# Turning normed rows by DMA instead of on TensorE in a fused attention and feed-forward kernel

## The chip, the cores and the metric

The kernel runs on one core of a Trainium2 chip. The metric is device time in microseconds for one launch, the median over several runs. One execution was also taken by the hardware profiler; durations of single instructions come from it. The engines are named as in the profile: PE is TensorE's matmul side and PEld its weight loads, DVE is VectorE, ACT is ScalarE, POOL is GpSimd, SP is SyncE, which here only issues DMAs.

## What is computed

Attention over hash buckets (4 batches, 8 heads, 768 positions, head size 64), followed by RMS norm and a gated feed-forward layer over 3072 tokens of width 512:

```python
q_bits = (np.einsum('bhsd,dk->bhsk', q, proj) > 0)      # 6 bits, a bucket each; k likewise
mask = q_bucket[:, :, :, None] == k_bucket[:, :, None, :]
scores = np.where(mask, scale * np.matmul(q, k.transpose(0, 1, 3, 2)), -1e9)
attn = softmax(scores)                                  # over keys
x = np.matmul(attn, v)                                  # to tokens x 512
xn = x / rms * rms_g
g = xn @ w_gate                                         # 512 -> 1536
return (silu(g) * (xn @ w_val)) @ w_out                 # 1536 -> 512
```

Inputs and output are float32.

## The kernel before

**Units.** The work is cut into 8 units: unit u is one half (384 positions) of batch u // 2, with all 8 heads. A unit's attention has 24 slots (`SLOTS`): 8 heads by 3 blocks of 256 keys. In a slot PE makes two score tiles of 128 keys by 384 queries (line 369), ACT takes their exponential into `p` (line 376), and PE multiplies `p` with the values into `pv` a slot and a half later (line 400; the last slot of a head pair adds a constant term, line 388).

**Order by hand.** Nothing is scheduled by the tool. Every step is put in a list with a position, `at(pos, fn)`, positions being counted in slots; the list is sorted by position and the steps are then issued in that order, so it sets the order on each engine. Each engine works its own instructions in order. A unit's base is 24 times its number; its norm and feed-forward part are laid over the attention of the next unit, whose base is `base = SLOTS * (u + 1)`.

**Norm of a unit** (`queue_norm`): `rstd` at base + 0.6 (DVE line 464, then POOL line 468), then three `scale` steps, one for each 128 tokens, 0.35 slots apart (DVE line 475), which write the normed rows `xn`, 128 tokens by 512 columns in float16. The gates need them turned, `xnT`, with the 512 columns on partitions in 4 groups of 128. `tr(0)` and `tr(1)` do that: each is 6 transposes of 128x128 on PE into a PSUM tile `xtp` of the pool `ring` (line 488), which DVE (line 494) or ACT (line 496) copies to `xnT`. For units 1 to 6 `tr(0)` is put 3.7 slots behind `rstd`.

**Gates** (`queue_gates`): 12 steps of a unit, each with 4 matmuls for the gate `g_ps` and 4 for the value `v_ps` (line 527), tanh on ACT (line 536), and two operations on DVE (lines 544 and 553) into `ht`. Every one of these matmuls reads all 384 tokens of `xnT`. Their PSUM tiles come from `gvpool`, which has 3 banks; a gate uses two. Positions are given in steps of F = 24 / 18 slots behind the base: 4, 5, 6, 7, 10, 11 and so on to 17 for units 1 to 5, and 4.45 for the first of unit 6.

**Output** (`queue_out`): 6 steps a unit of 6 matmuls each (line 591), over the slots of the unit after, at F-steps 0, 1, 2, 3, 8 and 9 for units 0 to 5; ACT copies out (line 601) and SP sends the unit out in one DMA (line 607).

**The next batch's q and k.** SP loads them a head pair at a time (`load_qk`, lines 71 and 72, 4 buffers each); PE turns them (line 226), a hash matmul in four column tiles of 32 gives the bits (line 240), and SP puts the bits, 6 rows at a time, into the scores' operands with small DMAs from SBUF to SBUF (`place`, line 259, 8 for a head pair). For batches 2 and 3 the four loads stand at 8 and 3 slots before the base and 2 and 7 after it; PE uses them from slots 0.4, 10.3, 24.4 and 32.3 behind that base.

**Opening.** While the first loads are under way PE multiplies zeros (`keep_warm`, line 107): 24 matmuls of 128x128 into a scratch tile, and a few more between the first real steps. The first of these turns head 0 of q (line 226).

Of the kernel before, what the change touches and what calls it, by code (L numbers as in the profile page):

```python
# [8 lines left out]
FP32 = mybir.dt.float32  # L9
# [13 lines left out]
HQ = 384  # L23
NU = 2 * B
# [9 lines left out]
def kernel(  # L34
# [12 lines left out]
    nc = tc.nc  # L47
# [5 lines left out]
    ring = ctx.enter_context(tc.tile_pool(name="ring", bufs=4, space=PSUM))  # L53
    pvpool = ctx.enter_context(tc.tile_pool(name="pvpool", bufs=1, space=PSUM))
    gvpool = ctx.enter_context(tc.tile_pool(name="gvpool", bufs=3, space=PSUM))
# [4 lines left out]
    def at(pos, fn):  # L60
        queue.append((pos, len(queue), fn))
# [5 lines left out]
    def load_qk(b, hp):  # L67
        ql = stage.tile([128, 2, 6, D], FP32, name="ql", tag="ql")
        kl = stage.tile([128, 2, 6, D], FP32, name="kl", tag="kl")
        hs = slice(2 * hp, 2 * hp + 2)  # L70
        nc.sync.dma_start(out=ql, in_=q[b, hs].rearrange("h (p c) d -> p h c d", c=6))
        nc.sync.dma_start(out=kl, in_=k[b, hs].rearrange("h (p c) d -> p h c d", c=6))
        loads[(b, hp)] = [ql, kl]
# [27 lines left out]
    zero = work.tile([128, HQ], FP16, name="zero", tag="bits", bufs=4)  # L101
    nc.vector.memset(zero, 0.0)
    wps = pvpool.tile([128, HQ], FP32, name="wps", tag="pv")

    def keep_warm(n):
        for _ in range(n):
            nc.tensor.matmul(  # L107
                wps[:, 0:128], zero[:, 0:128], zero[:, 0:128], start=True, stop=True
            )

    keep_warm(24)
    ident = const.tile([128, 128], FP32, name="ident")
    make_identity(nc, ident)
    NQK = 6
# [4 lines left out]
    for i in range(2):  # L119
        t = const.tile([128, 6, H, 65], FP16, name=f"v16_{i}")  # L120
# [6 lines left out]
    for e in range(2):  # L127
        t = const.tile([128, 32], FP32, name=f"pj1_{e}")
# [26 lines left out]
    for i in range(2):  # L155
        t = const.tile([128, NP, 1, 2, 65], BF16, name=f"vsum{i}")
# [171 lines left out]
    def queue_prep(b, hp, p0, step, hlag=0.3, eng=None, dpos=None):  # L328
        part = make_prep(b, hp)
        if (b, hp) == (1, 1):  # L330

            for j in range(4):
                pos = (24.56, 24.57, 26.6, 27.6)[j]
                part(pos, "tr_mm", j, (gvpool, "gv"))
                part(max(pos, 25.2), "tr_ev", j, "vvaa"[j])
            ph = 29.3
        else:
            for j in range(4):
                part(p0 + step * j, "tr_mm", j)
                part(p0 + step * j, "tr_ev", j, eng)  # L340
            ph = p0 + step * 4 + hlag
        part(ph, "hash_mm")
        part(ph, "bits")
        for i, (c, e) in enumerate(PLACES):
            part(ph + 0.001 * (i + 1), "place", c, e)
        for i, (c, e) in enumerate([(0, 0), (1, 0), (1, 1), (0, 1)]):
            part((dpos or ph + 0.7) + 1.33 * i, "dims", c, e)
        return part, ph
# [108 lines left out]
    xnT_of = {}  # L457

    def queue_norm(u, p, sgap, gap):
        tl = {}  # L460

        def rstd():
            ms = work.tile([128, 3], FP32, name="ms", tag="ms")
            nc.vector.tensor_scalar(  # L464
                ms, ss_of[u, 0], 1.0 / DMODEL, 1e-6, op0=ALU.mult, op1=ALU.add
            )
            rs = work.tile([128, 3], FP32, name="rs", tag="rs")
            nc.gpsimd.tensor_tensor(rs, ms, mhalf, op=ALU.pow)  # L468
            tl["rs"] = rs
            tl["xn"] = work.tile([128, 3, DMODEL], FP16, name="xn", tag="xn", bufs=1)  # L470
            xnT_of[u] = work.tile([128, 4, HQ], FP16, name="xnT", tag="xnT")

        def scale(t):
            def go():
                nc.vector.scalar_tensor_tensor(  # L475
                    out=tl["xn"][:, t, :], in0=x_of[u][:, t, :],
                    scalar=tl["rs"][:, t : t + 1], in1=grow,
                    op0=ALU.mult, op1=ALU.mult,
                )
            return go  # L480

        def tr(j):
            def go():
                m = ring.tile([128, 2, HQ], FP16, name="xtp", tag="r")
                for t in range(3):
                    for i in range(2):
                        kt = 2 * j + i
                        nc.tensor.transpose(  # L488
                            m[:, i, 128 * t : 128 * t + 128],
                            tl["xn"][:, t, 128 * kt : 128 * kt + 128],  # L490
                            ident16,
                        )
                if j == 0:
                    nc.vector.tensor_copy(xnT_of[u][:, 0:2, :], m)
                else:
                    nc.scalar.activation(xnT_of[u][:, 2:4, :], m, AF.Copy)  # L496
            return go

        at(p, rstd)
        for t in range(3):  # L500
            at(p + sgap + 0.35 * t, scale(t))
        at(p + gap, tr(0))
        at(p + gap + 0.35, tr(1))

# [210 lines left out]
    def qk_at(pos, b, hp):  # L715
        at(pos, lambda: load_qk(b, hp))

    def v_at(pos, part, b, hp):

        if (b, hp) != (1, 0):  # L720
            at(pos, lambda: load_v(b, hp))
        part(pos + 0.3, "vcast")
        part(pos + 0.31, "vsum")
# [6 lines left out]
    for b in range(1, B):  # L730
        base = SLOTS * (2 * b - 1)
        if b == 1:
            p0s = (17.3, None, base + SLOTS + 0.4, base + SLOTS + 8.3)
        else:
            p0s = (base + 0.4, base + 10.3, base + SLOTS + 0.4, base + SLOTS + 8.3)
            for hp in range(4):
                qk_at(base - 8.0 + 5.0 * hp, b, hp)
        parts = [
            queue_prep(
                b, hp, p0s[hp], 1.0,  # L740
                eng="v" if b == 1 and hp < 2 else None,
                dpos=(32.2, 37.5)[hp] if b == 1 and hp < 2 else None,
            )
            for hp in range(4)
        ]
        if b == 1:
            vps = [18.1, 30.2, 34.0, 38.0]
        else:
            vps = [parts[hp // 2][1] + 0.1 + 1.5 * (hp % 2) for hp in range(4)]
        for hp in range(4):  # L750
            v_at(vps[hp], parts[hp][0], b, hp)

    for u in range(NU):
        queue_attention(u, SLOTS * u, 1.0, 1.1 if u == 0 else 0.0)
        p = SLOTS * (u + 1) + 0.6
        if u == 0:
            queue_norm(u, p, 1.0, 6.2)
        else:
            queue_norm(u, p, 1.0, 3.7 if u < NU - 1 else 5.0)
    F = SLOTS / 18.0  # L760
    steps = lambda base, js: [base + 0.15 + F * j for j in js]
    for u in range(NU):
        base = SLOTS * (u + 1)
        if u == 0:
            queue_gates(u, [base + 8.0 + 1.33 * j for j in range(12)], 1.33)
        else:
            js = [4.0 if u < NU - 2 else 4.45, 5, 6, 7, 10, 11, 12, 13, 14, 15, 16, 17] if u < NU - 1 else range(6, 18)
            queue_gates(u, steps(base, js), F, u == NU - 1)
        js = [0, 1, 2, 3, 8, 9] if u < NU - 2 else range(6)
        queue_out(u, steps(base + SLOTS, js), u == NU - 1)  # L770

    for _, _, fn in sorted(queue, key=lambda e: (e[0], e[1])):
# [31 lines left out]
```

## Time and profile before

| what | us |
|---|---|
| median of 3 runs | 353.16 (352.51 to 353.35) |
| the profiled execution, its own time | 352.91 |
| its span | 351.1 |
| PE busy | 342.9 |
| ACT busy | 239.2 |
| DVE busy | 233.2 |
| scores, line 369 | 94.5 |
| gate and value matmuls, line 527 | 156.4 |
| output matmuls, line 591 | 68.7 |
| the `scale` steps, line 475 | 16.6 |

The span goes from the first to the last instruction that the profiler saw; the execution's own time is 1.8 us more. Busy times of matmuls overlap in the pipeline, so a group's mean is longer than the time it takes in PE's stream; the chain that ended last gives the latter. The granted TensorE clock is 0.998 over the span. In the timeline a row merges instructions of one kind that follow each other: start, length, engine, line, output and inputs, count, and in brackets the idle time of the engine before it with what ended it. "SPq" rows are issues of DMAs on SP's queue, not the transfers.

### The profile page before, as it was taken

How to read it: one execution, taken by the hardware profiler on the slowest of the kernel's cores; microseconds unless marked ns; L12 is line 12 of the kernel's file. 1: busy time of each engine (PE TensorE's matmuls, PEld its weight loads, DVE VectorE, ACT ScalarE, POOL GpSimd, SP SyncE). 2: the span in 40 equal slices, each digit the busy share in tenths (PEclk: the TensorE clock that was granted, in tenths of full speed). 3: DMA queues.
4: the chain of work that ended last, by engine and by line, in shares of the span. 5: the costliest groups of instructions: out<-in, count | busy, mean ns of one | idle time of the engine just before them, and what ended most of it. 6: DMA issues, size and time to landing. Idle time of an engine off the chain costs nothing.

```text
span 351.1 us, 8105 instructions
## 1 busy us (share of the span) xinstructions
PE 342.9 (98%) x3108; PEld 214.7 (61%) x3108; DVE 233.2 (66%) x493; ACT 239.2 (68%) x547; POOL 70.3 (20%) x112
## 2 busy tenths in 40 slices
PE   8998999999999999999999999999999999999996
PEld 6555665666666666666656656666666655665653
DVE  5667888677574784766767675767758644575771
ACT  4868877777677676777777677676767676772421
POOL 3899700820000006050000005051000000000000
PEclk9999999999999999999999999999999999999999
DMA  7956999500028016200008206220002000200202
GB/s 249 377 176 89 201 252 206 127 2 4 2 74 292 2 65 211 95 1 3 6 3 271 93 3 183 96 90 2 8 1 95 0 2 2 91 2 1 91 0 90
DMA packets 24054, 31.21 MB, mean 89 GB/s; under 512 B 2096, under 2 KB 20944, under 8 KB 24016
## 3 DMA queue, kind: packets, MB, share of 16 engines
q1 hardware_dynamic: 17792, 25.65, 21.9%
q0 software_dynamic: 5824, 4.72, 8.9%
q8 instruction: 24, 0.39, 0.4%
q10 hardware_dynamic: 400, 0.34, 0.3%
q14 instruction: 14, 0.11, 0.1%
HBM read 28.58 MB, written 6.29 MB: 99 GB/s over the span
## 4 chain that ended last, share of the span: by engine, by line
PE 94%; DVE 2%; ACT 2%; issue 1%; ACTq 0%; DVEq 0%
PE v_ps L527 18%; PE o_ps L591 18%; PE g_ps L527 17%; PE s_ps L369 17%; PE pv L400 10%; PE trps L226 6%; PE hps L240 3%; PE xtp L488 1%; PE pv L388 1%; ACT p L376 1%; PE hps L269 1%; PE wps L107 1%; DVE x L417 1%; ACT xnT L496 0%; DVE qk L276 0%
## 5 line engine op out<-in xcount | busy, mean ns | idle before, releaser
L376 ACT ACTIVATE p<-s_ps 128x384 f16<-128x384 f32 x384 | 162.9, 496 | 53.4 <-PE s_ps L369 52.9
L369 PE MATMUL s_ps<-qk 71*128 71x384 f16 x384 | 94.5, 326 | 0.4 <-ACT xnT L496 0.2
L527 PE MATMUL v_ps<-xnT,wv 128*128 128x384 f16 x384 | 78.1, 326 | 1.1 <-DVE a L544 1.1
L527 PE MATMUL g_ps<-xnT,wg 128*128 128x384 f16 x384 | 78.3, 325 | 0.1
L544 DVE SCALAR_TENSOR_TENSOR a<-th,g_ps 128x384 f32<-128x384 f32 x96 | 53.1, 553 | 33.1 <-ACT th L536 31.6
L400 PEld LDWEIGHTS <-p 128*128 128x128 f16 x1152 | 59.4, 97 | 24.6 <-issue 2.2
L591 PE MATMUL o_ps<-wo,ht 128*128 128x512 f16 (+1 forms) x300 | 68.7, 370 | 0.0
L400 PE MATMUL pv<-v,p 128*128 128x65 f16 x1152 | 66.2, 193 | 0.9 <-DVE x L417 0.7
L536 ACT ACTIVATE th<-g_ps 128x384 f32<-128x384 f32 x96 | 48.0, 499 | 17.6 <-PE g_ps L527 15.7
L553 DVE TENSOR_TENSOR ht<-a,v_ps 128x384 f16<-128x384 f32 x96 | 53.1, 553 | 8.4
L527 PEld LDWEIGHTS <-wv 128*128 128x128 f16 x384 | 37.5, 98 | 26.3 <-issue 1.6
L527 PEld LDWEIGHTS <-wg 128*128 128x128 f16 x384 | 35.1, 97 | 22.8 <-issue 2.3
L591 PEld LDWEIGHTS <-ht 128*128 128x128 f16 x300 | 28.2, 97 | 26.4
L468 POOL TENSOR_TENSOR rs<-ms,mhalf 128x3 f32<-128x3 f32 x8 | 6.9, 860 | 172.6 <-DVE ms L464 172.6
L369 PEld LDWEIGHTS <-qk 71*128 71x128 f16 x384 | 28.2, 98 | 14.2 <-issue 6.9
L601 ACT ACTIVATE osb<-o_ps 128x512 f32<-128x512 f32 (+1 forms) x23 | 13.5, 588 | 23.9 <-PE o_ps L591 23.9
L304 POOL CAST v<-vl 128x768 f16<-128x768 f32 x16 | 13.3, 834 | 67.7 <-DMA vl<-in_v_dram 45.0
L416 DVE RECIPROCAL r<-pv 128x6 f32<-128x6 f32 x32 | 6.2, 195 | 31.0 <-PE pv L400 30.8
L235 DVE TENSOR_SCALAR kT<-trps 128x384 f32<-128x384 f32 x28 | 15.5, 552 | 11.7 <-PE trps L226 11.7
L233 ACT ACTIVATE qT<-trps 128x384 f32<-128x384 f32 x29 | 14.4, 496 | 9.1 <-PE trps L226 9.1
L475 DVE SCALAR_TENSOR_TENSOR xn<-x,rs,grow 128x512 f16<-128x512 f32 x24 | 16.6, 748 | 4.6 <-POOL rs L468 4.6
L430 DVE CUSTOM_DVE_ANT_0 sq<-x 128x512 bf16<-128x512 f32 (+2 forms) x33 | 18.9, 571 | 0.9
(68 smaller groups left out, 272.6 us busy)
## 6 DMA issues: line engine op xcount, KB each, us to landing
vl<-in_v_dram SPq DMA_DIRECT2D x16, 384.0 KB
ql<-in_q_dram SPq DMA_DIRECT2D x15, 384.0 KB
kl<-in_k_dram SPq DMA_DIRECT2D x15, 384.0 KB
out_dram<-osb SPq DMA_DIRECT2D x7, 768.0 KB
qk<-bits SPq DMA_DIRECT2D x112, 4.5 KB
wg<-in_moe_w_gate_dram POOLq DMA_DIRECT2D x4, 384.0 KB, 6.8
wv<-in_moe_w_val_dram POOLq DMA_DIRECT2D x4, 384.0 KB, 9.3
wo<-in_moe_w_out_dram POOLq DMA_DIRECT2D x4, 384.0 KB, 13.2
```

What stands on the lines that cost most here:

```text
L226: nc.tensor.transpose(m[:, i, :], src[:, i, :], ident)
L235: nc.vector.tensor_scalar_mul(dst, mm, DIM)
L369: nc.tensor.matmul(s_ps, qk[0:71, 2 + hh, 128 * jt : 128 * jt + 128], qk[0:71, hh, HQ * hf : HQ * hf + HQ], start=True, stop=True,)
L376: nc.scalar.activation(p, s_ps, AF.Exp, scale=SCL)
L400: nc.tensor.matmul(acc[:, t, hh, :], p[:, 128 * t : 128 * t + 128], v16s[b % 2][:, 2 * (jt % 3) + jt // 3, h, :], start=(n % 6 == 0 and i ...
L430: nc.vector.tensor_tensor_reduce(out=sq[:, lo:hi], in0=xs, in1=xs, scale=1.0, scalar=0.0, op0=ALU.mult, op1=ALU.add, accum_out=ss_of[u, pa ...
L475: nc.vector.scalar_tensor_tensor(out=tl["xn"][:, t, :], in0=x_of[u][:, t, :], scalar=tl["rs"][:, t : t + 1], in1=grow, op0=ALU.mult, op1=A ...
L527: nc.tensor.matmul(ps, w[:, kt, fs], xnT[:, kt, :], start=(kt == 0), stop=(kt == 3))
L536: nc.scalar.activation(th, tl[f][0], AF.Tanh, scale=0.5)
L544: nc.vector.scalar_tensor_tensor(out=a, in0=th, scalar=1.0, in1=g_ps, op0=ALU.add, op1=ALU.mult)
L553: nc.vector.tensor_mul(ht_of[u][f], a, v_ps)
L591: nc.tensor.matmul(acc, ht_of[u][f][:, 128 * t : 128 * t + 128], wo[:, f, lo:hi], start=(f == 0), stop=(f == 11),)
```

## The change

For units 1 to 6, `queue_norm` no longer issues `tr(0)` and `tr(1)`. Behind each `scale` step stands one transposing DMA on SP's queue that reads 128 tokens by 512 columns of `xn` in SBUF and writes them, turned, to `xnT` in SBUF. No PSUM tile, no PE instruction and no copy on DVE or ACT is left in it. Units 0 and 7 keep the transposes on PE. The gates of units 1 to 6 start one F-step later (unit 6: 0.55 of a step), and the later ones are closer together, ending at 17.2 steps in place of 17. The last two output steps of units 0 to 5 are a step later. The loads of q and k for batches 2 and 3 stand at 8 and 3.5 slots before the base and 4.5 and 9 after it.

In the opening, 12 of the 24 zeros are replaced: two rounds, each with two matmuls whose operands are 64 rows high and four that are 32 rows high, of 384 columns, each row tile with its own PSUM tile, followed by 2 of the old kind.

```diff
-    keep_warm(24)
+    keep_warm(8)
+    parts_of = [
+        (gvpool if g % 2 else ring).tile(
+            [128, HQ], FP32, name="wps", tag="gv" if g % 2 else "r"
+        )
+        for g in range(4)
+    ]
+    for _ in range(2):
+        for rows in (64, 32):
+            for g in range(128 // rows):
+                z = zero[rows * g : rows * g + rows]
+                nc.tensor.matmul(parts_of[g], z[:, 0:128], z, start=True, stop=True)
+        keep_warm(2)
...
+        def tr_dma(t):
+            def go():
+                nc.sync.dma_start_transpose(
+                    out=xnT_of[u][:, :, 128 * t : 128 * t + 128], in_=tl["xn"][:, t, :]
+                )
+            return go
+
         at(p, rstd)
         for t in range(3):
             at(p + sgap + 0.35 * t, scale(t))
+        if 0 < u < NU - 1:
+            for t in range(3):
+                at(p + sgap + 0.35 * t + 0.01, tr_dma(t))
+            return
         at(p + gap, tr(0))
         at(p + gap + 0.35, tr(1))
...
-                qk_at(base - 8.0 + 5.0 * hp, b, hp)
+                qk_at(base + (-8.0, -3.5, 4.5, 9.0)[hp], b, hp)
...
-            js = [4.0 if u < NU - 2 else 4.45, 5, 6, 7, 10, 11, 12, 13, 14, 15, 16, 17] if u < NU - 1 else range(6, 18)
+            js = [5.0, 5.9, 6.9, 7.9, 10.9, 11.8, 12.7, 13.6, 14.5, 15.4, 16.3, 17.2] if u < NU - 1 else range(6, 18)
             queue_gates(u, steps(base, js), F, u == NU - 1)
-        js = [0, 1, 2, 3, 8, 9] if u < NU - 2 else range(6)
+        js = [0, 1, 2, 3, 9, 10] if u < NU - 2 else range(6)
```

## The prediction

> **What bounds the kernel now.** I read the page first: busy time by engine, then the shares of the chain that ended last.
>
> ```profile
> PE 342.9 (98%) x3108; PEld 214.7 (61%) x3108; DVE 233.2 (66%) x493; ACT 239.2 (68%) x547; POOL 70.3 (20%) x112
> ...
> PE 94%; DVE 2%; ACT 2%; issue 1%; ACTq 0%; DVEq 0%
> ```
>
> TensorE is 94% of the chain; DVE and ACT have a third of the span free. What leaves PE's stream shortens the run by its pace on PE, and any wait put into that stream lengthens it in full.
>
> Next, the view of the tile xtp, the transposes' PSUM target:
>
> ```profile
> L488 PE MATMUL xtp<-ident,xn x96: 217/219/230, 43.9 to 322.8; 128*128 128x128 f16 x96
> L494 DVE COPY xnT<-xtp x8: 547/558/559, 44.8 to 322.7; 128x768 f16<-128x768 f16 x8
> L496 ACT ACTIVATE xnT<-xtp x8: 810/810/818, 45.4 to 323.0; 128x768 f16<-128x768 f16 x8
> ```
>
> The 219 ns is one pipelined matmul's length, not its price. The chain in order of time gives line 488 1.5% of the span, 5.27 us for 96 transposes: 0.055 us each.
>
> Then the timeline where unit 1 is normed (start, length):
>
> ```profile
> 76.95 2.08 DVE L475 SCALAR_TENSOR_TENSOR xn<-x,rs,grow 128x512 f16<-128x512 f32 x3 [0.53 <-POOL rs L468]
> ...
> 79.31 0.50 PE L488 MATMUL xtp<-ident,xn 128*128 128x128 f16 x6
> ...
> 81.37 0.81 PE L527 MATMUL g_ps<-xnT,wg 128*128 128x384 f16 x4
> ...
> 81.76 1.50 SPq L259 DMA_DIRECT2D qk<-bits  x2
> ```
>
> and of unit 6, where PE does wait for the ACT copy:
>
> ```profile
> 282.32 2.08 DVE L475 SCALAR_TENSOR_TENSOR xn<-x,rs,grow 128x512 f16<-128x512 f32 x3 [0.96 <-POOL rs L468]
> ...
> 284.71 0.50 PE L488 MATMUL xtp<-ident,xn 128*128 128x128 f16 x6
> ...
> 286.79 0.81 PE L527 MATMUL g_ps<-xnT,wg 128*128 128x384 f16 x4
> ```
>
> The reader is to see how little lies between the last xn row (79.03; 284.40) and the first gate: 2.3 us. Units 2 to 5 repeat unit 1 with the same spacings, 41.35 us apart.
>
> Last, the opening, and bytes moved just after the first place DMA:
>
> ```profile
> 1.18 2.74 PE L107 MATMUL wps<-zero 128*128 128x128 f16 x24 [1.18 <-DVE pj L129]
> ...
> 3.86 0.87 PE L226 MATMUL trps<-ident,ql 128*128 128x128 f32 x3
> ```
> ```profile
> 82.75:83.00 0.25, 0.25 (x8) 0.21 (x7) 0.25 (x1) 0.00 (x0) 0.00 (x0) 1.00 0.00 0
> 83.00:83.25 0.25, 0.25 (x4) 0.16 (x2) 0.25 (x1) 0.00 (x0) 0.00 (x0) 1.00 0.07 19
> ```
>
> PE goes from the zeros straight into the first transposes, so a longer opening is on the path. The place DMA (SBUF to SBUF) began to issue at 81.76; its bytes moved in the slice from 83.00 to 83.25, 1.24 to 1.49 us later. That is my nearest row for a transposing DMA.
>
> **The change, part by part.** The sum is made against the profiled execution, 352.91 us (span 351.1); the median of the runs is 353.16, so 0.25 is added at the end.
>
> *Transposes off PE.* Six units of 12: 72 x 0.055 = 3.95 us off the bound engine. The six DVE copies (0.56) and ACT copies (0.81) go too; off the chain these are worth nothing, save in unit 6. There, from 284.71 to 286.79, 2.08 us pass for work that runs elsewhere at 12 transposes 0.66, two PV groups 2 x 0.18, two pairs of scores 2 x 0.33 = 1.68; the other 0.40 is the wait for the ACT copy. It goes: -0.40. In unit 1 the same count leaves 0.1; I book nothing.
>
> *The new wait.* PE's first gate of a unit now waits for three transposing DMAs, and PE is in order: all of attention queues behind it. When is it reached? In the changed order, what stands between the output matmuls and that gate is PV, hash, a score pair, PV, a score pair, PV with its constant. From 79.31: 0.18 + 0.79 + 0.33 + 0.18 + 0.33 + 0.35 puts the gate at 81.47. In unit 6 it is PV, scores, PV, scores, PV with constant: 284.71 + 1.37 = 286.08. When does the last transpose land? Its xn row ends at 79.03; SP follows DVE by 0.03 (bits end 81.73, place 81.76); 1.24 to 1.49 for a small DMA; and 128 KB at the 337 to 418 GB/s of the last output DMAs, 0.31 to 0.39. So 80.6 to 80.95: covered by 0.5 to 0.9 us in units 1 to 5. In unit 6, 284.43 + 1.55 to 1.88 = 286.0 to 286.3: a wait of 0 to 0.2; I take 0.2. SP can keep up if an issue takes the 0.66 us of a place DMA, against 0.69 us per xn row. No row shows a transposing DMA; the far bound is the 6.8 us from issue to landing of the weight loads on POOL's queue: 79.06 + 6.8 is 4.4 late, 284.43 + 6.8 is 5.15 late, 27 us in all. I take the near row, since payload, memory and queue are its kind.
>
> [...]
>
> *SP's queue.* 18 DMAs more. Behind each three stand the next head pair's places (first at 81.76 in unit 1; SP would be free by 79.7) and loads. Two of the q/k loads go from 2 and 7 slots after the unit's start to 4.5 and 9, behind the transposes; their tiles are used from slot 24.4, some 35 us later at 1.72 us a slot. Output steps 4 and 5 go a step later; their DMA is waited for a unit later. Nothing for these; without that cover a late load would stall PE by its delay.
>
> *Gates closer together.* Gates 4 to 11 keep their end but start later: 0.9 of a step apart instead of 1. PE waits for DVE to free a gate bank twice now, 1.1 us in all, at most 0.7. Bounds: 0 (DVE has 34% free and loses a copy) and one 0.7 wait per unit, 4.2; I take 0.5, nearer to the present two in eight units.
>
> *The zeros.* 24 zeros take 2.74 us, 0.114 per 128 columns. Twelve of them become matmuls of 384 columns, in four groups of 2 or 4 row tiles. If the tiles of a group run at once, four passes of 0.34 replace 12 x 0.114: equal. If one after another, 12 x 0.34 less 1.37: +2.74. Row tiles show in no row; the nearest, the hash's column tiles, do run together (four within 0.03 us of each other). I take +0.3 for tile starts; it could be -0.5 if PE's pace (0.055 per 128 columns later) came sooner.
>
> Sum: -3.95 - 0.40 + 0.2 + 0.5 + 0.3 = -3.35. 352.91 - 3.35 + 0.25 = **349.8 us**.
>
> **The rivals.** *The transposes follow one another* (slower). If each transposing DMA starts only when the one before has landed, with 1.7 us each from 77.67, the third lands at 82.8: 1.3 late, and in unit 6 283.04 + 5.1 is 2.1 late. 5 x 1.3 + 2.1 = 8.7 in place of 0.2: 358.1. For it: three DMAs on one path, and xn rows come every 0.69. Against: SP's place DMAs go out 0.72 to 0.75 apart, though each moves 1.2 later. It decides from d us each where 5(3d - 3.80) + (3d - 3.04) exceeds the rest's gain of 3.55: d = 1.42.
>
> *Each transpose costs SP by its 128-column blocks*: 12 issues of 0.66 from 77.67, then 0.7 to land, 86.3: 4.8 late, unit 6 5.6, together 29.7: 379 us. For it: a place of 4.5 KB costs SP more (0.66) than a load of 384 KB (0.42), so issue isn't priced by bytes. Against: a load of 256 runs of 1.5 KB costs SP less than a place of 6 runs, so issue isn't priced by pieces in these rows.
>
> *Row tiles don't run together*: +2.74 for 0.3, 352.2. *Closer gates wait once each unit*: 4.2 for 0.5, 353.5. In both the change moves the time by less than can be told.
>
> **How the numbers follow.** A measurement of this kernel can't tell 0.3%, 1.06 us, from no change: faster is below 352.1, slower above 354.2. Forecast 0.50, its own range 348.3 (waits nil, opening -0.5) to 352; transposes one after another 0.25; by blocks 0.10; row tiles in turn 0.10; waiting gates 0.05. A little of the second case has d below 1.42, which gives faster 0.53, same 0.13, slower 0.34. The range runs from 348.3 to 360, the second case up to d of about 1.8, and leaves out its tail and the blocks.
>
> **What would show it.** No line 488 for six units, and so a quarter of its share in the chain. The first gate of units 1 to 5 starting about 2.4 us after the last xn row, with no idle PE ahead of it released by a DMA; in unit 6 idle of 0.2 at most. SP issues of transposes near 0.66 us. The zeros ending near 4.2. Wrong is the forecast if PE sits idle ahead of line 527's first gate six times, by more than 0.6 each.

## The result and the profile after

The changed kernel takes 366.06 us (363.32 to 369.12) against 353.13: a ratio of 1.034, interval 1.031 to 1.038, which leaves out the one slow run, 369.12. It is slower by some 13 us; 3.4 faster was forecast. The profiled execution took 365.97 us.

Of the page of the changed kernel, busy time by engine and the shares of the chain:

```profile
PE 345.8 (95%) x3036; PEld 211.9 (58%) x3036; DVE 230.2 (63%) x487; ACT 235.0 (65%) x541; POOL 70.3 (19%) x112
...
PE 89%; DMA 4%; DVE 4%; ACT 2%; issue 1%; ACTq 0%; DVEq 0%
```

PE has 72 instructions fewer, is busy for 2.9 us longer and idle for 18.4 us where it was 8.2. "DMA" is new in the chain. The timeline at unit 1's norm shows where:

```profile
77.47 2.08 DVE L488 SCALAR_TENSOR_TENSOR xn<-x,rs,grow 128x512 f16<-128x512 f32 x3 [0.53 <-POOL rs L481]
...
78.25 3.92 SPq L514 DMA_TRANSPOSE xnT<-xn  x3
...
81.99 0.53 PE L413 MATMUL pv<-v,p 128*128 128x65 f16 x6
...
83.58 0.81 PE L551 MATMUL g_ps<-xnT,wg 128*128 128x384 f16 x4 [1.07 <-DMA xnT<-xn]
```

The xn rows are done at 79.55, 0.69 apart. SP needs 3.92 us for its three issues; the chain puts the last one's start at 80.95, 1.4 us behind its rows. The view of the tile xnT, and that chain from its start to the gate (start, length):

```profile
L514 SPq DMA_TRANSPOSE xnT<-xn x18: 1200/1225/2232, 78.2 to 296.4; - x18
```
```profile
80.95 2.50 DMA xnT<-xn
83.45 0.14 issue
83.58 0.81 PE g_ps L551 x4
```

Issue to landing is 2.50 us, of which the bytes take about 0.6: in the DMA view from 76 to 86 us, in 40 slices of 0.25 us, each of the three transfers fills some three slices near 200 GB/s.

```profile
GB/s 0 66 0 0 0 0 0 0 0 0 0 0 0 0 150 219 153 3 0 96 214 199 16 0 46 216 213 50 0 0 19 0 0 19 0 0 15 3 0 19
```

PE's waits (in all, times, longest) and, by stretches of 3.41 us, PE's busy time and its granted clock (next to last before the two DMA columns) around the late gates of units 3, 4 and 6:

```profile
PE g_ps L551 <- DMA xnT<-xn: 8.8, 6, 2.5
PE v_ps L551 <- DVE a L568: 2.6, 7, 0.4
```
```profile
166.11:169.52 3.41, 1.93 (x23) 1.13 (x20) 2.23 (x5) 1.64 (x4) 0.00 (x0) 1.00 0.41 79
169.52:172.94 3.42, 3.42 (x17) 1.71 (x16) 1.56 (x3) 1.15 (x3) 0.00 (x0) 0.50 0.02 6
210.48:213.89 3.41, 2.11 (x25) 0.95 (x17) 2.23 (x5) 1.86 (x5) 0.00 (x0) 1.00 0.52 57
213.89:217.30 3.41, 2.22 (x19) 1.46 (x20) 0.74 (x2) 0.99 (x3) 0.00 (x0) 1.00 0.74 227
295.82:299.23 3.41, 1.55 (x19) 0.88 (x17) 0.76 (x2) 1.87 (x5) 0.00 (x0) 1.00 0.39 77
299.23:302.65 3.42, 3.42 (x18) 1.76 (x17) 1.11 (x2) 1.21 (x3) 0.00 (x0) 0.50 0.02 5
```

After 1.48 and 1.86 us of idle PE in one stretch, the clock is at half in the next; unit 4's longer wait is split over two stretches, 1.30 and 1.19, and nothing follows. The opening is the last piece (before, the turn of q began at 3.86):

```profile
1.18 1.03 PE L107 MATMUL wps<-zero 128*128 128x128 f16 x8 [1.18 <-DVE pj L142]
...
2.15 0.94 PE L123 MATMUL wps<-zero 64*128 64x384 f16 x6
...
4.42 0.84 PE L239 MATMUL trps<-ident,ql 128*128 128x128 f32 x3
```

### The profile page after: what moved, and what is told of

Read it like the earlier page. It is cut to its first block, busy times and chain, and to the rows that moved or that the text cites. A ratio compares the mean times of both kernels' runs of the same rounds, so it can differ in the third digit from the quotient of the medians.

```text
span 364.2 us, 8001 instructions
## 1 busy us (share of the span) xinstructions
PE 345.8 (95%) x3036; PEld 211.9 (58%) x3036; DVE 230.2 (63%) x487; ACT 235.0 (65%) x541; POOL 70.3 (19%) x112
## 4 chain that ended last, share of the span: by engine, by line
PE 89%; DMA 4%; DVE 4%; ACT 2%; issue 1%; ACTq 0%; DVEq 0%
PE v_ps L551 18%; PE o_ps L615 17%; PE g_ps L551 16%; PE s_ps L382 15%; PE pv L413 9%; PE trps L239 6%; DMA xnT<-xn 4%; PE hps L253 3%; DVE x L430 1%; ACT p L389 1%; PE hps L282 1%; PE pv L401 1%; DVE a L568 1%; PE wps L107 1%; DVE r L429 0%
## 5 line engine op out<-in xcount | busy, mean ns | idle before, releaser
L382 PE MATMUL s_ps<-qk 71*128 71x384 f16 x384 | 95.9, 329 | 0.1
L551 PE MATMUL g_ps<-xnT,wg 128*128 128x384 f16 x384 | 79.1, 328 | 8.9 <-DMA xnT<-xn 8.8
L551 PE MATMUL v_ps<-xnT,wv 128*128 128x384 f16 x384 | 79.4, 330 | 2.6 <-DVE a L568 2.6
L413 PEld LDWEIGHTS <-p 128*128 128x128 f16 x1152 | 60.3, 98 | 28.2 <-issue 2.9
L413 PE MATMUL pv<-v,p 128*128 128x65 f16 x1152 | 67.7, 194 | 1.1 <-DVE x L430 0.7
```

Of the source, the lines that this page charges most:

```text
L382: nc.tensor.matmul(s_ps, qk[0:71, 2 + hh, 128 * jt : 128 * jt + 128], qk[0:71, hh, HQ * hf : HQ * hf + HQ], start=True, stop=True,)
L413: nc.tensor.matmul(acc[:, t, hh, :], p[:, 128 * t : 128 * t + 128], v16s[b % 2][:, 2 * (jt % 3) + jt // 3, h, :], start=(n % 6 == 0 and i ...
L551: nc.tensor.matmul(ps, w[:, kt, fs], xnT[:, kt, :], start=(kt == 0), stop=(kt == 3))
```

## The experiments

"Ratio" is to the kernel before on the same chip, with its 95% interval. The kernel before took 352.99 us on the chip of the first four experiments, 353.33 on that of the next four and 353.07 on that of the last three; each difference to it is taken on its own chip.

### The opening alone

The kernel before, with the change's zeros:

```diff
-    keep_warm(24)
+    keep_warm(8)
...
+    for _ in range(2):
+        for rows in (64, 32):
+            for g in range(128 // rows):
...
+        keep_warm(2)
```

> The kernel before with the new opening alone. In the trace of the changed kernel the first turn of q starts at 4.42 us instead of 3.86 and the first norm 0.5 us later. Theory 1 (the row tiles of a group run at once, and the opening is on the path): +0.5 us, about 353.6. Rival (PE's later steps absorb it, for the loads set the pace by then): 353.1, no change. Second rival (row tiles use PE's clock up and slow what follows): more than +1 us.

353.47 us, ratio 1.0016 (1.0007 to 1.0025): +0.5 us, as the first theory had it. Six row tiles of 384 columns take about 0.9 us (2.15 to 3.03 in the changed kernel), against two passes of 0.34 (three times the 0.114 of a zero of 128 columns) if a group's tiles ran fully at once and six if in turn. They overlap, but not fully: 0.2 us a round is lost, and the delay stays to the end.

### The positions alone

The kernel before, transposes on PE:

```diff
-            js = [4.0 if u < NU - 2 else 4.45, 5, 6, 7, 10, 11, 12, 13, 14, 15, 16, 17] if u < NU - 1 else range(6, 18)
+            js = [5.0, 5.9, 6.9, 7.9, 10.9, 11.8, 12.7, 13.6, 14.5, 15.4, 16.3, 17.2] if u < NU - 1 else range(6, 18)
...
-        js = [0, 1, 2, 3, 8, 9] if u < NU - 2 else range(6)
+        js = [0, 1, 2, 3, 9, 10] if u < NU - 2 else range(6)
...
-                qk_at(base - 8.0 + 5.0 * hp, b, hp)
+                qk_at(base + (-8.0, -3.5, 4.5, 9.0)[hp], b, hp)
```

> The kernel before, transposes on PE, with the changed positions of gates, output steps and q/k loads alone. In the changed kernel PE's waits ahead of v_ps are about 0.45 us longer in each of units 1 to 6. Theory 1 (gates 0.9 of a step apart run into the three gate banks by themselves): +2.5 to +3.5 us, about 356, with the waits of v_ps for DVE at line 544 growing from 1.1 to 3 or 4 us. Rival (those waits come only from the bunching after the stall for the transposes): within 0.5 us of 353.1.

356.81 us, ratio 1.0109 (1.0096 to 1.0123): +3.8 us, a little above the expected range, with waits that grow less than expected. PE's waits for DVE in the kernel before and in this one:

```profile
PE v_ps L527 <- DVE a L544: 1.1, 2, 0.7
```
```profile
PE v_ps L527 <- DVE a L544: 2.6, 7, 0.4
```

The same 2.6 us in 7 waits as in the changed kernel, without any transposing DMA: they belong to the positions. The rows show 1.5 us more of such waits than before; a unit has become 0.7 us longer (xn rows of units 1 and 2 42.05 us apart, before 41.32), so the larger part of the 3.8 us lies in matmuls that start late without an idle row. Gates, output steps and loads moved together; which of them costs what was not measured.

### Output steps first

The changed kernel with other positions:

```diff
-            js = [5.0, 5.9, 6.9, 7.9, 10.9, 11.8, 12.7, 13.6, 14.5, 15.4, 16.3, 17.2] if u < NU - 1 else range(6, 18)
+            js = range(6, 18)
...
-        js = [0, 1, 2, 3, 9, 10] if u < NU - 2 else range(6)
+        js = range(6)
```

> The changed kernel with the output steps of the unit before at F-steps 0 to 5 and the gates at 6 to 17, one step apart, for all units: two output steps (2.6 us on PE) and some attention now stand ahead of the first gate, which is then reached some 6 us after the last xn row; the third transpose lands 3.9 us after it, in the worst unit 5.4. Theory 1 (PE lost its time waiting for the landing, in gates too close together and in the clock that fell after the idle time): no wait for xnT, no fall of the clock, the transposes' 3.95 us gained: about 349.5 to 350.5. Rival (a transposing DMA under way slows other work, or the later gates pile up against the unit's end): 355 or more, the loss showing in other waits.

350.44 us, ratio 0.9931 (0.9918 to 0.9943). The timeline of its unit 1:

```profile
78.17 2.08 DVE L488 SCALAR_TENSOR_TENSOR xn<-x,rs,grow 128x512 f16<-128x512 f32 x3 [0.53 <-POOL rs L481]
...
78.95 3.92 SPq L514 DMA_TRANSPOSE xnT<-xn  x3
...
86.21 0.81 PE L551 MATMUL g_ps<-xnT,wg 128*128 128x384 f16 x4
```

SP's issues are as slow as ever, but the gate is reached 6.0 us behind the xn rows, and no wait for xnT is left.

### Six issues of half the size

```diff
-                nc.sync.dma_start_transpose(
-                    out=xnT_of[u][:, :, 128 * t : 128 * t + 128], in_=tl["xn"][:, t, :]
-                )
+                for c in (0, 2):
+                    nc.sync.dma_start_transpose(
+                        out=xnT_of[u][:, c : c + 2, 128 * t : 128 * t + 128],
+                        in_=tl["xn"][:, t, 128 * c : 128 * c + 256],
+                    )
```

> The changed kernel with each transposing DMA cut into two of 256 columns, six a unit. Measures what an issue on SP (1.22 us for 512 columns) is made of. Theory 1 (SP pays by the block that it pushes): about 0.65 us an issue, six in some 4 us, the gate's wait as in the changed kernel or 0.3 us longer, 366 to 368 us. Rival (a fixed price for each transposing DMA): 1.2 us each, six in 7.5 us, the gate 3.5 us later in each of six units, some 385 us or more.

392.61 us in a single run (before 352.99). The view of its tile xnT and its timeline at unit 1:

```profile
L515 SPq DMA_TRANSPOSE xnT<-xn x36: 1190/1230/2094, 78.4 to 322.9; - x36
```
```profile
78.44 7.72 SPq L515 DMA_TRANSPOSE xnT<-xn  x6
86.12 0.80 PE L553 MATMUL g_ps<-xnT,wg 128*128 128x384 f16 x2 [3.41 <-DMA xnT<-xn]
```

The rival holds: half the columns cost SP the same, 1.23 us for 256 against 1.22 for 512, so at these two sizes the price is one for the instruction.

### PE kept busy during the wait

The changed kernel with spare matmuls, whose results are thrown away, ahead of the first gate:

```diff
+                if f == 0 and 0 < u < NU - 1:
+                    fill = ring.tile([128, HQ], FP32, name="fill", tag="r")
+                    for _ in range(20):
+                        nc.tensor.matmul(
+                            fill[:, 0:128], ident16, ident16, start=True, stop=True
+                        )
```

> The changed kernel with 20 spare matmuls of 128x128 (1.1 us at 0.055) on PE just ahead of the first gate of units 1 to 6, so that PE is busy in most of the time in which it waits for the transposes; they are thrown away. In the changed kernel the granted clock fell to 0.5 for 3.4 us behind the gates of units 3 and 6, and its runs go with their mean clock: 363.3 and 364.0 at 0.995, 366.0 to 366.4 at 0.990, 369.1 at 0.986. Theory 1 (the fall follows the idle time and costs some 2 us each): no fall or one at most, clock 0.997 or more, about 361.5 to 362.5, runs closer together, the wait for the transposes ending at the same time after the xn rows. Rival (the clock falls for another cause, such as the transposing DMAs themselves): falls as before, 365 to 368.

361.35 us (360.99 to 361.45), ratio 1.0227 (1.0213 to 1.0241), granted clock 1.000: 4.7 us less than the changed kernel by the medians, 4.1 by the two ratios, with 120 matmuls more, and runs within 0.5 us instead of 3 or more. The stretches at unit 3's gate, which were at 1.00 and then 0.50 in the changed kernel:

```profile
165.80:169.20 3.40, 3.39 (x49) 2.36 (x42) 2.23 (x5) 1.68 (x5) 0.00 (x0) 1.00 0.40 79
169.20:172.60 3.40, 3.40 (x33) 2.32 (x32) 1.81 (x4) 2.51 (x6) 0.00 (x0) 1.00 0.02 6
```

The transposing DMAs are the same and the idle time is filled, and no fall is left (1.000 over the span, 0.991 in the changed kernel): here the clock fell with the idle time. Not all of the difference is the clock: in the profiled executions the gates of units 3 and 4 are also 1.5 us less late here (3.94 and 4.49 us behind their rows; 4.45 and 5.47 there).

### Output steps first, transposes on PE

The kernel before with `js = range(6, 18)` for the gates and `js = range(6)` for the output steps.

> The kernel before, transposes on PE, with output steps at F-steps 0 to 5 and gates at 6 to 17 in all units: what the positions of the third experiment bring by themselves. Theory 1 (they bring nothing, the gain there is the transposes' PE time): 352.5 to 354, so that the DMA's transposes are worth 3 us or more at these positions. Rival (the gain came from the order of gates and outputs): 350.4 to 351.

354.32 us, ratio 1.0031 (1.0020 to 1.0042). The positions of gates and output steps don't bring the gain; they cost 1 us.

### The same with the old opening

The third experiment with `keep_warm(24)`.

> The third experiment (transposing DMAs, output steps first, gates from step 6) with the old opening of 24 zeros. Theory 1 (the new opening's 0.5 us adds as it did on the kernel before): 349.9, faster than both kernels. Rival (the later order takes it up): 350.4, as with the new opening.

350.01 us, ratio 0.9908 (0.9894 to 0.9921): faster than both kernels. Against the experiment before it, on the same chip and with gates and output steps at the same positions, it gains 354.32 - 350.01 = 4.3 us. The loads of q and k are at their new places here and at the old ones there, so this is not the transposes alone. PE's busy time is: 344.7 us there, 340.5 here, 4.2 less.

### One transposing DMA a unit

```diff
-            for t in range(3):
-                at(p + sgap + 0.35 * t + 0.01, tr_dma(t))
+            at(p + sgap + 0.71, tr_dma)
...
+            nc.sync.dma_start_transpose(out=xnT_of[u], in_=tl["xn"])
...
+            shape = [128, 12, 128] if 0 < u < NU - 1 else [128, 4, HQ]
```

> The changed kernel, positions and opening as they are, with one transposing DMA of 128 by 1536 for a unit in place of three of 128 by 512, behind the third xn row; xnT is kept with the tokens' tile as its outer index. An issue took 1.2 us whatever its size (256 or 512 columns), 1.35 from one to the next, so the third issued 1.3 us behind its rows. Theory 1 (the lateness is the fixed issue price taken three times): one issue 0.1 us behind the third row, landing 2.5 us after that or up to 1 us more for three times the bytes, the wait at the first gate 0 to 1 us instead of 1.2 to 2.9: 357 to 361. Rival (the time is in the transfer, 128 KB each, so that 384 KB last three times as long): issue to landing 5 us or more, the gate as late as now: 366 or more.

363.34 us, ratio 1.0290 (1.0276 to 1.0305), between the two theories. The view of its xnT and the chain at unit 1:

```profile
L514 SPq DMA_TRANSPOSE xnT<-xn x6: 1479/1492/1673, 79.8 to 293.7; - x6
```
```profile
79.77 3.77 DMA xnT<-xn
```

The issue starts right behind the rows (79.74), 1.4 us sooner than the third of three, but 384 KB land 3.8 us later instead of 2.5. The gate gains 0.2 us: 3.8 us behind the rows for 4.0. So it is in five of the six units; in unit 5 the landing takes 5.0 us; why stays open. Three times the bytes cost 1.3 us more, 0.6 for each further 128 KB, as in the slices above. Issues in series and transfer are here two ways to the same lateness; some 1.9 us beside the bytes (2.50 less 0.6, 3.77 less three times 0.6) are left in either.

### The transposes' swap alone

The kernel before with `tr_dma` for `tr` in units 1 to 6, all else as it was.

> The kernel before with the transposes of units 1 to 6 as three DMAs and nothing else changed: old opening, gates, output steps and loads. Without the transposes PE reaches the first gate some 1.7 us after the last xn row, and the third DMA lands 3.9 after it. Theory 1 (lateness of the landing, plus the fall of the clock, less 3.95): waits of 2.2 in units 1 to 5 and 1.7 in unit 6, less 3.95 and the 0.4 of the ACT copy, is +8.4, with two to four falls of the clock at some 2 us each: 365 to 371. So the later gates of the change bought back about what their closer spacing costs. Rival (waits are made good later, for the other engines run ahead meanwhile): 358 or less.

379.86 us, ratio 1.0756 (1.0733 to 1.0779), 9 us beyond the expected range. PE's waits:

```profile
PE g_ps L539 <- DMA xnT<-xn: 20.8, 6, 6.3
```

In units 1, 3, 5 and 6 the gate starts 3.9 to 4.2 us behind the rows, as expected; in units 2 and 4 it is 7.2 and 8.1. Only there do q/k loads stand among the transposes. The clock falls more often than expected, too: the profile has seven stretches at half pace, at most 12 us of PE's work, against two in the changed kernel; the granted clock is 0.967 over the span, 0.991 there.

### The loads at their old places

The seventh experiment with `qk_at(base - 8.0 + 5.0 * hp, b, hp)`.

> The seventh experiment (transposing DMAs, output steps first, old opening) with the q/k loads at their old places, the third pair's two loads 0.4 slots behind the transposes instead of 2.9. Theory 1 (with 2 us of cover at the gate the loads' place makes no difference): 350.0, within 0.5. Rival (loads share the DMA path with the transposes and hold them up past the gate): 352 or more, with waits for xnT in units 2 and 4.

351.18 us, ratio 0.9944 (0.9930 to 0.9958), against 0.9908 (0.9894 to 0.9921) without this edit. The time lies between the two theories; the waits for xnT, 2.6 us in units 2 and 4, are the rival's. SP's queue at unit 2:

```profile
118.88 2.77 SPq L502 DMA_TRANSPOSE xnT<-xn  x2
121.74 0.54 SPq L71 DMA_DIRECT2D ql<-in_q_dram  x1
122.37 0.41 SPq L72 DMA_DIRECT2D kl<-in_k_dram  x1
122.88 1.19 SPq L502 DMA_TRANSPOSE xnT<-xn  x1
```

Slot 2.0 lies between the second and the third transpose, not 0.4 slots behind it. The third is issued behind 768 KB of loads, and its gate starts at 127.31, 4.4 us after that issue began instead of 2.5. PE's busy time is the seventh experiment's, 340.5 us, so against the sixth, whose loads are at the same old places, the transposes take the same 4.2 us off PE and the loads' place gives part of it back as waits.

### Five output steps ahead

The seventh experiment with gates at `[5.5, 6.5, 7.5, 8.5, 9.5, 10.4, 12.2, 13.2, 14.2, 15.1, 16.1, 17.1]` up to unit 5 and output steps at `[0, 1, 2, 3, 4, 11.3]` up to unit 4.

> As the seventh experiment, but five output steps ahead of the gates instead of six, the sixth at step 11.3, and the first gate at 5.5, so that it is reached some 4.5 us after the last xn row. Theory 1 (three issues and the landing take 3.9 us in most units, up to 5.4 when an issue lasts longer): no waits in most units, one of up to 1 us in some; 349.5 to 351. Rival (the order with the output steps first cost 1 us on PE before, and this order does not): 349.

358.11 us, ratio 1.0143 (1.0129 to 1.0157): both missed.

```profile
PE g_ps L539 <- DVE a L556: 5.1, 5, 1.3
PE v_ps L539 <- DVE ht L565: 1.4, 2, 0.7
...
PE g_ps L539 <- DMA xnT<-xn: 1.0, 2, 0.5
```

The landing is nearly covered, as the first theory had it; the new waits are for `gvpool`'s three banks, which the moved output step and gates also share.

## Why the prediction was wrong

*The step that failed is the landing of the last transpose*: "80.6 to 80.95: covered by 0.5 to 0.9 us in units 1 to 5". Three parts of it were too small. An issue was taken as 0.66 us, a place DMA's; it is 1.22, and three follow 1.35 apart, so the third starts 1.4 us behind its rows. Issue to landing was 1.55 to 1.88 us; it is 2.50, for I read the slice in which bytes moved as the landing. And 128 KB move at some 200 GB/s, not the 337 to 418 of the output. Together the last transpose lands 3.9 us behind its rows where I had 1.6 to 1.9. The gate was forecast 2.4 us behind the rows; in unit 1 the PV group ahead of it starts at 81.99, so PE is there about 2.8 behind them. The six waits are of 1.0 to 2.5 us, above the 0.6 that the prediction names as its sign of being wrong.

*The rival "the transposes follow one another" had the right lateness.* It put the third landing at 82.8 in the old timeline, 1.3 late; measured are 83.45, or 82.9 less the opening's 0.5, and a gate waiting 1.07. Not by its mechanism, though, so the match is luck: here the second DMA does not wait for the landing of the first (it is issued at 79.66, and the first, issued at 78.25, would land at 80.75 with the third's 2.50); SP is busy issuing. Its sum is 358.3, not 358.1, with the 0.25 that the forecast adds for the median. It fell 8 us short because of three sums that it shared with the forecast:

- *Closer gates*: 0.5 taken of 0 to 4.2; alone, with the output steps and loads that moved with them, they cost 3.8. "Nearer to the present two" was the wrong row to choose by: it counts waits of gates a full step apart.
- *The clock*: not in the sum at all. Two stretches of 3.41 us at half pace lose at most 3.4 us of PE's work. In the changed kernel's trace the clock is 0.50 from 169.52 to 172.94 us and from 299.23 to 302.65, behind stretches with 1.48 and 1.86 us of idle PE; behind unit 4's 1.30 and 1.19 it stays at 1.00. Where the border lies is not shown: the longest wait for xnT in the tenth experiment is 1.5 us, and its clock is 1.000 over the span.
- *Late issues*: the second issues of units 3 and 4 lasted 1.73 and 2.23 us. Why stays open; the longest issue of the fourth experiment lasted 2.09, of the eighth, which has one a unit, 1.67.

*Right*: the PE time. 3.95 and 0.40 were forecast for the transposes and the ACT copy; between the sixth and the seventh experiment PE's busy time falls by 4.2 us and the median by 4.3. The opening was 0.3 forecast, 0.5 measured, row tiles overlapping. SP's loads: "nothing for these" looked only at who uses the loads; the move out from among the transposes is worth 1 us even where the gate has 2 us of cover. Where it has none it is probably worth more, as the ninth experiment's units 2 and 4 suggest; that was not measured alone.

A sum by measured parts: -4.3 for PE, +0.5 opening, +3.8 positions, then the wait at six gates and the fall of the clock. The fifth experiment, with a clock of 1.000, leaves 361.35 - 353.33 + 4.3 - 0.5 - 3.8 = 8.0 for the waits, near the 8.8 that the changed kernel's trace shows; the rest up to the changed kernel, 4 to 5 us, is put down to the clock with the later issues of units 3 and 4. How much each of the two has was not measured apart.

## What to carry to other kernels

Where one engine is 94% of the chain, taking work off it can pay that work, here 4.2 us, but only if the result is back before the engine gets there: count issue, transfer and landing from the last producer, and put as much of the bound engine's other work in between, as the output steps here. Price an unknown DMA from its landing signal at a consumer, not from when bytes move (here 2.50 us against the 0.6 of the bytes), and count issues of one queue in series (here 1.35 us apart). A wait on PE can cost twice, once as idle time and again as a slower clock after it: the changed kernel waits 8.8 us for xnT and then has two stretches of 3.41 us at half clock.

## What had not been expected

- A transposing DMA costs SP 1.23 us for 256 columns, 1.22 for 512 and 1.49 for 1536; plain DMAs of the same queue mostly 0.4 to 0.7 (medians by line in the changed kernel: v 0.39, k 0.47, q 0.49, output 0.64, places 0.66).
- In the changed kernel's trace PE's clock fell to half for 3.41 us behind 1.48 and 1.86 us of idle PE within one stretch of that length, and did not behind 1.30 and 1.19. That kernel's runs spread over 3 us or more with their mean clock (363.3 us at 0.995, 366.4 at 0.990), those of the kernel before within 1.
